# Sixty-four wide tiles in an attention recurrence with segment memory: output products in one pass, scores in one tile shape, a new order of the work

## The chip, the core and the metric

The kernel runs on one core of one Trainium2 chip. TensorE (PE in the profile, with PEld for its weight loads) multiplies, VectorE (DVE), ScalarE (ACT) and GpSimd (POOL) do the rest, and SyncE (SP) issues most of the transfers. The metric is the device time in microseconds of one execution; lower is better.

## The reference

All tensors are bfloat16. The sequence has 2048 tokens of 640 channels, cut into 64 segments of 32 tokens. Each segment is put behind 8 memory tokens, and attention with 32 heads of 192 channels runs over these 40 rows. The first 8 rows of its output are the memory of the next segment, so the segments form a chain. Beside it runs a gated feed-forward layer over all tokens, and a gate mixes the two.

```python
def _A_ref(x, mem0, Wq, Wk, Wv, Wo, seg_len):
    ...
    idx = jnp.arange(L)
    mask = (idx[:, None] < M) | (idx[:, None] >= idx[None, :])
    mem = mem0
    outs = []
    for s in range(n_seg):
        xs = x[:, s * seg_len:(s + 1) * seg_len, :].copy()
        h = jnp.concatenate([mem, xs], axis=1)
        q = jnp.einsum('btd,dhe->bhte', h, Wq)
        k = jnp.einsum('btd,dhe->bhte', h, Wk)
        v = jnp.einsum('btd,dhe->bhte', h, Wv)
        scores = jnp.einsum('bhqe,bhke->bhqk', q, k) * scale
        scores = jnp.where(mask[None, None], scores, -1000000000.0)
        p = _softmax(scores, axis=-1)
        o = jnp.einsum('bhqk,bhke->bhqe', p, v)
        o = jnp.einsum('bhte,hed->btd', o, Wo)
        mem = o[:, :M, :].copy()
        outs.append(o[:, M:, :])
    return jnp.concatenate(outs, axis=1)
...
g = _sigmoid((x * gate_w).sum(-1, keepdims=True))
a = _A_ref(x, A_mem0, A_Wq, A_Wk, A_Wv, A_Wo, A_seg_len)
b = _B_ref(x, B_w_gate, B_w_up, B_w_down)
return g * a + (1 - g) * b
```

## The kernel before

**Stages.** The feed-forward layer comes first (the lines up to 830 or so, some 175 us with the first left rows); its result waits in a scratch tensor. Then the 64 segments run, one after the other. Every operation goes through a recorder (`_Sched`): it lists operations with the regions that they read and write, and derives all waits from these. Each engine runs its own list in order, so the order in which operations are recorded is the order of every queue: TensorE's, VectorE's, ScalarE's, GpSimd's and SP's.

**Rows.** A segment has 40 rows, but a 32-wide tile of TensorE holds 32. The kernel therefore keeps 32 *main* rows (8 memory tokens and the first 24 tokens) and 8 *left* rows (the last 8 tokens). The left rows do not depend on the chain. Those of four segments make a *group*: 32 left rows, whose Q and K are projected ahead, during the group before (`lf` for the matmuls, `le` for eviction, two transposes on VectorE and a store to a scratch tensor, read back by `stg_load` in the segment that needs it). A segment's place in its group, its number modulo 4, is called its position, `q`.

**Heads.** 32 heads go as four octets. Per octet: projections of Q, K and V, each five steps of K (`g` in the order, `proj`, lines 1046 and 226, four matmuls of 32 rows and 384 columns side by side; line 226 is the form that keeps the weights of the matmul before); eviction by ScalarE (L1066, L1069) and transposes of Q and K by VectorE (`tq` and `tk`, L1080); scores (`sc`, L1087 mask, L1095 and L1100); the softmax (L1112 and L1114 with the scores, `ex` with L1124 to L1131); transposed probabilities (`pt`, L1144 and L1149, evicted by L1162 or L1156 with L1158); their product with V (`pv`, L1177 and L1179, evicted into `uT` by L1188 and L1193); and the product with Wo (`wo`, two halves of two pairs each).

A head has 192 channels. Two heads make a pair of 384 = 3 x 128, so the middle 128 hold the ends of both heads: the scores take two 128-row matmuls and two half-height ones for each pair.

**Output.** The first three octets' products with Wo run as four 32-wide tiles, each with 320 columns (L1206): two pairs of heads times two halves of the columns, summed afterwards by one ScalarE copy (`Zp`, L1212) and two VectorE additions (`Zs`, L1215). The last octet's are four tiles of 160 columns (L1229) in bank `OB2`. `Z evac` (L1371) adds both, and L1375 transposes the result into the next segment's input. In position 3 the same Wo pieces also multiply the group's 32 left rows, gathered from four segments in `uTl`, in bank `LB` (`wo_left`, L1206 as well); the last part of it runs after the transposes. `left_sums` adds the halves in the next segment and mixes the rows.

**Weights.** Of 60 Wq, Wk and Wv pieces and 16 Wo pieces most stay in SBUF. 16 places are shared by two pieces each: 13 pieces of the first and the last octet and 3 Wo pairs. Segments run the octets forwards and backwards in turn. When the first user of a place is done, `swap_loads` records on SP the load of its partner (L599), needed at the end of the same segment. SP also issues the loads and stores of the left rows, of the feed-forward rows and of the output, in the same queue.

**The order** is written out by hand in two lists: `GROUPS`, which projections share a step, and `PROG`, the order of all items of a segment. One `PROG` serves all positions; `lf`, `le` and `vb` items act only in the position that they name.

```python
    def segment(s):
        ...
        for n, item in enumerate(PROG):
            kind, i = item[0], item[1]
            ...
            swap_loads(s, item)
```

Of the kernel before, what the change touches and what calls it, by code (L numbers as in the profile page):

```python
# [230 lines left out]

def _build(nc, A_x, A_mem0, A_Wq, A_Wk, A_Wv, A_Wo, seg_len, w_gate, w_up, w_down,
# [46 lines left out]
    total = int(nc.sbuf_bytes_remaining) - 64  # L279
# [8 lines left out]
    wsA["xs"] = al(KT * XA * 2)  # L288
    wsA["gall"] = al(NSEG * 4)
    wsA["gallL"] = al(32 * 4)  # L290
    wsA["ident"] = al(128 * 2)
    wsA["maskm"] = al(R * 2)
    wsA["elw"] = al(2 * 7 * 16 * 2)
    wsA["XLg"] = 2 * al(KT * 32 * 2)
    NVB, NUB = 2, 2
# [7 lines left out]
    wsB["uT"] = al(NUB * 12 * R * 2)  # L303
    wsB["stats"] = al(2 * 3 * 4 * 4 + 8)
    wsB["p"] = al(4 * 64 * 2)
    wsB["uTl"] = al(NCH * 32 * 2)
# [63 lines left out]
    gallL = fview(wsA_off["gallL"], 128)  # L370
    r_gallL = sreg(wsA_off["gallL"], 128)
# [5 lines left out]
    elw = bview(wsA_off["elw"], 448).rearrange("p (i b r) -> p i b r", i=2, r=16)  # L377
    r_elw = sreg(wsA_off["elw"], 448)
# [4 lines left out]
    r_Ql = sreg(wsB_off["Q"] + 8, 12 * R * 2 - 8)  # L383
    Ks = bview(wsB_off["K"], 12 * R * 2).rearrange("p (s r) -> p s r", r=R)
# [4 lines left out]
    stg_off = (wsB_off["stg"], wsB_off["uT"] + 24 * R)  # L389
    assert 8 * LW <= 24 * R  # L390
# [23 lines left out]
    r_uTp = [[sreg(wsB_off["uT"] + b * UB, 4), sreg(wsB_off["uT"] + b * UB + 4, 4)] for b in range(NUB)]  # L414
    st_f = [[fview(wsB_off["stats"] + (3 * b + i) * 16, 16) for i in range(3)] for b in range(2)]
    r_st = [sreg(wsB_off["stats"] + 48 * b, 48) for b in range(2)]
    uTl = bview(wsB_off["uTl"], NCH * 64).rearrange("p (c t) -> p c t", t=32)
    r_uTl = [sreg(wsB_off["uTl"] + 12 * 64 * b, 12 * 64) for b in range(NOCT)]
    bz, bzl = [bview(wsB_off[nm], DJ * 2) for nm in ("bz", "bzl")]
    Zt = PT[:, 0:DJ]  # L420
    r_bzlj = [sreg(wsB_off["bzl"], DJ * 2, 32 * j, 32 * j + 32) for j in range(4)]
# [8 lines left out]
    fp_sz = {"xst": 16 * KT * XA * 2, "xls": 4 * KT * 64, "gr": 512 + 4 * NSEG + 128, "gwT": 64}  # L430
# [13 lines left out]
    r_gin = [sreg(o_gr + 512, 4 * NSEG, 32 * j, 32 * j + 32) for j in range(4)]  # L444
    ginL = fview(o_gr + 512 + 4 * NSEG, 128)
# [54 lines left out]
    def piece_view(key, o):  # L500
        if key[0] == 3:
# [3 lines left out]
    GROUPS = [[(0, 0), (1, 0)], [(2, 0), (0, 1), (1, 1)], [(2, 1), (0, 2)], [(1, 2)], [(2, 2), (0, 3)], [(1, 3)], [(2, 3)]]  # L505
    PROG = [("g", 0, 0), ("g", 0, 1), ("g", 0, 2), ("g", 0, 3), ("g", 0, 4), ("tq", 0), ("g", 1, 0), ("tk", 0),
# [27 lines left out]
    def seg_order(s):  # L534
        keys = []
        for item in PROG:
# [6 lines left out]
    orders = [seg_order(0), seg_order(1)]  # L543
# [20 lines left out]
    o = 0  # L564
# [37 lines left out]
    def piece(seg, key):  # L602
        order = orders[seg % 2]
# [42 lines left out]
    def asel(ap, reg, pattern, base, cm, fill):  # L646
# [9 lines left out]
    S_.add("pool", lambda e: e.memset(elw[:, :, 3, :], 1.0), writes=[r_elw])  # L656
    S_.add("pool", lambda e: e.affine_select(out=elw[:, :, 3, :], in_=elw[:, :, 3, :], pattern=[[-64, 2], [-1, 16]],
                                             compare_op=ALU.is_equal, fill=0.0, base=-XA, channel_multiplier=1),
           reads=[r_elw], writes=[r_elw])
# [204 lines left out]
    gate_loads()  # L864
    load_residents(2)

    S_.add("pool", lambda e: e.memset(pl_sb, 0.0), writes=[r_p])
    lb = {}
    LBK = {}

# [600 lines left out]
```

## Time and profile before

| | us |
|---|---|
| median of 3 runs | 1765.19 (1756.74 to 3865.19) |
| the profiled execution, its span | 1765.1 |
| TensorE's clock in it, mean share of full speed | 0.994 |
| L1046 and L226, projections, busy | 723.0 and 595.4 |
| L1206, output products of 320 columns, busy | 293.6 (6144 matmuls) |
| L1229, those of 160 columns, busy | 74.0 (3072) |
| L1095 and L1100, scores, busy | 69.3 and 70.8 (2048 each) |
| L1080, transposes of Q and K on VectorE, busy, mean of one | 270.8, 0.557 |
| L1215, half sums on VectorE, busy | 50.8 (160) |
| L1196, copies of the left rows on GpSimd, busy | 68.3 (256) |
| DMA, mean | 283 GB/s |

A busy time of TensorE is the time in which at least one matmul of the line ran. Matmuls in different columns of the array run beside each other, so the steps from start to start tell more than the lengths. The third run (3865.19) lies far off the other two.

### The profile page before, as it was taken

To read this page: it belongs to the slowest core of one execution; us is meant where nothing else is said; L and a number is where in the kernel's file an instruction comes from. 1 tells how busy PE (TensorE), PEld (TensorE's weight loads), DVE (VectorE), ACT (ScalarE), POOL (GpSimd) and SP (SyncE) were. 2 spreads that over 40 slices of the span, in tenths; PEclk is the share of its full clock that TensorE was granted. 3 is DMA by queue.
4 is the path that set the end of the run, shared out by engine and by line. 5 is a ranking of instruction groups with operands and counts; after the bars stand their busy time and mean duration, and the time that the engine had idled before them with its cause. 6 is when DMAs were issued, how large, how long until landed. Compare 5 with 4: busy or idle time off the path is not lost.

```text
span 1765.1 us, 80301 instructions
## 1 busy us (share of the span) xinstructions
PE 1623.9 (92%) x39162; PEld 809.5 (46%) x31501; DVE 960.0 (54%) x2932; ACT 802.8 (45%) x1835; POOL 320.0 (18%) x1099
## 2 busy tenths in 40 slices
PE   9999999999999999999999989999999998999887
PEld 4554444444444444454444444454444444454444
DVE  2222655556555655555555655555555655655554
ACT  3222544545444544444444544444444544445443
POOL 1100111111112112111212111111211121121211
PEclk9999999999999999999999999999999999999999
DMA  9814987888778887888788887879787886879776
GB/s 335 295 48 157 329 313 250 320 313 288 280 269 311 299 308 253 315 290 319 281 280 293 296 293 250 314 285 323 279 280 275 311 310 241 312 282 327 283 275 238
DMA packets 271311, 499.57 MB, mean 283 GB/s; under 512 B 105304, under 2 KB 132208, under 8 KB 270960
## 3 DMA queue, kind: packets, MB, share of 16 engines
q1 hardware_dynamic: 267832, 491.34, 78.3%
q8 instruction: 276, 4.52, 1.0%
q10 hardware_dynamic: 3128, 3.09, 0.6%
q14 instruction: 75, 0.61, 0.1%
HBM read 473.22 MB, written 21.11 MB: 280 GB/s over the span
## 4 chain that ended last, share of the span: by engine, by line
PE 71%; DVE 15%; DMA 6%; issue 4%; ACT 4%; DVEq 0%; SPq 0%; ACTq 0%
PE ps L1046 20%; PE ps L226 15%; PE ps L1206 8%; DMA arena<-in_A_Wo_dram 5%; PE ps L1177 3%; PE ps L804 3%; PE ps L801 3%; PE ps L884 3%; PE ps L1100 3%; PE ps L819 2%; PE ps L1087 2%; DVE ps L1114 2%; DVE arena L1112 2%; PE ps L1095 2%; PE ps L1229 2%
## 5 line engine op out<-in xcount | busy, mean ns | idle before, releaser
L1046 PE MATMUL ps<-arena 128*32 128x384 bf16 x9940 | 723.0, 329 | 42.4 <-DVE arena L1375 34.4
L226 PE MATMUL ps<-arena 128*32 128x384 bf16 x7680 | 595.4, 328 | 7.9 <-DVE arena L1215 3.5
L1046 PEld LDWEIGHTS ps<-arena 128*32 128x32 bf16 x9940 | 257.5, 97 | 365.3 <-issue 226.0
L1080 DVE STREAM_TRANSPOSE arena<-arena 128x384 bf16<-128x384 bf16 x512 | 270.8, 557 | 150.8 <-ACT arena L1066 149.2
L1066 ACT ACTIVATE arena<-ps 128x384 bf16<-128x384 f32 x512 | 236.2, 489 | 211.6 <-PE ps L1046 196.3
L1206 PE MATMUL ps<-arena 128*32 128x320 bf16 x6144 | 293.6, 301 | 13.9 <-issue 13.4
L1124 ACT ACTIVATE ps<-ps 104x160 f32<-104x160 f32 x256 | 71.9, 281 | 293.4 <-DVE ps L1114 293.4
L1206 PEld LDWEIGHTS ps<-arena 128*32 128x32 bf16 x6144 | 163.5, 97 | 74.0 <-issue 19.4
L1112 DVE TENSOR_REDUCE arena<-ps 104x4 f32<-104x160 f32 x256 | 83.0, 324 | 165.8 <-PE ps L1100 164.6
L941 POOL COPY arena<-arena 128x96 bf16<-128x96 bf16 x256 | 70.3, 275 | 513.4 <-PE ps L1100 444.2
L1188 ACT ACTIVATE arena<-ps 128x480 bf16<-128x480 f32 (+1 forms) x256 | 137.0, 535 | 43.8 <-PE ps L1179 39.6
L1196 POOL COPY arena<-arena 128x96 bf16<-128x96 bf16 x256 | 68.3, 267 | 441.1 <-ACT arena L1188 357.3
L1162 ACT ACTIVATE arena<-ps 128x448 bf16<-128x448 f32 x192 | 104.2, 543 | 96.7 <-PE ps L1149 96.4
L1069 ACT ACTIVATE arena<-ps 128x384 bf16<-128x384 f32 x256 | 125.1, 489 | 20.9 <-PE ps L1046 16.3
L1177 PE MATMUL ps<-arena 128*64 128x160 bf16 x1536 | 123.1, 243 | 12.5 <-ACT arena L1162 6.9
L1126 DVE TENSOR_REDUCE arena<-ps 104x4 f32<-104x160 f32 x256 | 83.0, 324 | 92.5 <-ACT ps L1124 92.5
L1177 PEld LDWEIGHTS ps<-arena 128*64 128x64 bf16 x1536 | 80.8, 109 | 91.6 <-issue 31.7
L884 PE MATMUL ps<-arena 128*32 128x384 bf16 x1280 | 111.4, 330 | 2.2 <-issue 2.0
L1179 PE MATMUL ps<-arena 128*64 128x64 bf16 x1536 | 104.8, 193 | 4.1 <-issue 4.1
L891 DVE STREAM_TRANSPOSE arena<-arena 128x384 bf16<-128x384 bf16 x128 | 73.7, 576 | 31.6 <-ACT arena L889 27.8
L1215 DVE TENSOR_TENSOR arena<-ps,arena 64x160 f32<-64x160 f32 x160 | 50.8, 317 | 72.3 <-ACT arena L1212 61.6
L1114 DVE TENSOR_TENSOR ps<-ps,arena 104x160 f32<-104x160 f32 x256 | 85.0, 332 | 8.8
(84 smaller groups left out, 1819.2 us busy)
## 6 DMA issues: line engine op xcount, KB each, us to landing
arena<-in_A_Wk_dram SPq DMA_DIRECT2D x335, 384.0 KB, 7.1
arena<-in_A_Wv_dram SPq DMA_DIRECT2D x335, 384.0 KB, 9.1
arena<-in_A_Wo_dram SPq DMA_DIRECT2D x205, 480.0 KB, 6.4
arena<-in_A_Wq_dram SPq DMA_DIRECT2D x209, 384.0 KB, 5.4
arena<-left_qk_scratch SPq DMA_DIRECT2D x126, 96.0 KB, 2.8
left_qk_scratch<-arena SPq DMA_DIRECT2D x49, 192.0 KB, 2.3
left_qk_scratch<-arena SPq DMA_DIRECT2D x30, 96.0 KB, 5.7
ffn_b_scratch<-arena ACTq DMA_DIRECT2D x16, 160.0 KB, 4.4
```

What stands on the lines that cost most here:

```text
L226: return e.add_instruction(mybir.InstMatmult(name=nm, start_tensor_calc=like["start"], stop_tensor_calc=stop, tile_size=(128, 32), tile_po ...
L884: fns.append(lambda e, outp=outp, rhs=rhs, j=j: e.matmul(outp, lhs, rhs, start=(k == 0), stop=(k == KT - 1), tile_position=(0, 32 * j)))
L1046: fns.append(lambda e, outp=outp, rhs=rhs, j=j: e.matmul(outp, lhs, rhs, start=(k == 0), stop=(k == KT - 1), tile_position=(0, 32 * j)))
L1066: S_.add("act", lambda e, m=m, bk=bk: e.activation(out=rows_sb[m], in_=ps[:, bk, 0:384], func=ACTF.Copy), reads=[r_ps[bk]], writes=[r_rows ...
L1069: S_.add("act", lambda e, i=i, bk=bk: e.activation(out=v_sb[i % NVB].rearrange("p (c n) -> p c n", c=3), in_=ps[:, bk, 0:384].rearrange("p ...
L1080: S_.add("dve", lambda e: e.transpose(out=dst[:, :, 0:L], in_=rows_sb[m].rearrange("p (c r) -> p c r", r=L)), reads=[r_rows[m]], writes=[r ...
L1112: S_.add("dve", lambda e: e.tensor_reduce(out=mxs, in_=S3, axis=AX.X, op=ALU.max), reads=[rb], writes=[rst], name="smax max")
L1114: S_.add("dve", lambda e: e.tensor_tensor(out=S3, in0=S3, in1=mxb, op=ALU.subtract), reads=[rb, rst], writes=[rb], name="smax sub")
L1177: return [lambda e: e.matmul(full, v[:, e0:e0 + 64], PTm[:, i], start=True, stop=False, tile_position=(0, 64 * i), skip_group_check=True), ...
L1179: lambda e: e.matmul(part, vl[:, e0:e0 + 64], PTl[:, i], start=False, stop=True, tile_position=(0, 64 * i), skip_group_check=True)]
L1188: S_.add("act", lambda e: e.activation(out=apx(u[:, 0, 0, :], [[R, na], [3 * R, 4], [1, R]]), in_=ps[:, A, 0:na * W].rearrange("p (c t r) ...
L1206: fns.append(lambda e, i=i, t=t, j=j, gv=gv: e.matmul(ps[32 * j:32 * j + 32, bank, 0:2 * DJ].rearrange("p (h n) -> p h n", h=2), lhs2[i], ...
```

## The change

**Scores.** The half-height matmuls ran in 64x64 tiles, one on the upper and one on the lower 64 rows. Now both are 128x64 tiles like the other scores. The upper one is issued with 64 rows of operands in a 128x64 tile (`_matmul_rows`). The lower one has all 128 rows, with `Qz` as its weights: a copy of Q's lower half by GpSimd, with zeros above it.

**Output products.** In position 3, main and left rows share one pass (`wo_both`): 64 weights (32 main, 32 left rows, side by side in `U3`), two tiles of 128x64 with 320 columns each. `U3l` on GpSimd puts the left rows there. Each bank row then holds a finished sum, so `Zp` and `Zs` fall away in position 3, and four operations take the place of the half sums of the left rows (`left_sums`). `Zq evac` (two by VectorE, two by ScalarE) gathers the main rows. In the other positions `Zs` is recorded after the last `pv` instead of before it. `uTl` now holds the left rows of three positions (24 columns), and left rows are loaded and stored in two parts, since their order in the bank changed.

**Order.** Six projection groups instead of seven: K of octet 2 joins V 1 and Q 2. Position 3 has an order of its own, `PROG3`. Both lists are new.

```diff
+def _matmul_rows(e, out, lhsT, rhs, start, stop, tile_position):
+    nm = e.bass.get_next_instruction_name()
+    return e.add_instruction(mybir.InstMatmult(
+        name=nm, start_tensor_calc=start, stop_tensor_calc=stop, tile_size=(128, 64), tile_position=tile_position,
+        bass_skip_group_check=True, ins=[e.lower_ap(rhs), e.lower_ap(lhsT)], outs=[e.lower_ap(out)]))
...
-    GROUPS = [[(0, 0), (1, 0)], [(2, 0), (0, 1), (1, 1)], [(2, 1), (0, 2)], [(1, 2)], [(2, 2), (0, 3)], [(1, 3)], [(2, 3)]]
+    GROUPS = [[(0, 0), (1, 0)], [(2, 0), (0, 1), (1, 1)], [(2, 1), (0, 2), (1, 2)], [(2, 2), (0, 3)], [(1, 3)], [(2, 3)]]
...
+    PROG = [("g", 0, 0), ("g", 0, 1), ("g", 0, 2), ("g", 0, 3), ("g", 0, 4), ("tq", 0), ("g", 1, 0), ("g", 1, 1),
+            ("tk", 0), ("g", 1, 2), ("sc", 0), ("g", 1, 3), ("ex", 0), ("g", 1, 4), ("g", 2, 0), ("g", 2, 1),
+            ("g", 2, 2), ("lf", 1, 0, 0), ("pt", 0), ("tq", 1), ("tk", 1), ("sc", 1), ("g", 2, 3), ("g", 2, 4),
+            ("tq", 2), ("ex", 1), ("lf", 2, 1, 0), ("lf", 1, 0, 1), ("lf", 1, 0, 2), ("pv", 0), ("g", 3, 0),
+            ("tk", 2), ("g", 3, 1), ("g", 3, 2), ("g", 3, 3), ("pt", 1), ("lf", 2, 1, 1), ("g", 3, 4), ("sc", 2),
...
+            ("pt", 3), ("lf", 0, 1, 2), ("wo", 2, 1), ("pv", 3), ("lf", 1, 1, 4), ("lf", 0, 1, 3), ("lf", 0, 1, 4),
+            ("le", 0, 1, 0), ("lf", 2, 1, 4), ("le", 2, 1, 0), ("le", 0, 1, 1), ("le", 1, 1, 0), ("le", 1, 1, 1),
+            ("wo", 3, 0), ("le", 2, 1, 1), ("wo", 3, 1)]
...
+            ("tk", 1), ("g", 2, 1), ("g", 2, 2), ("g", 2, 3), ("g", 2, 4), ("sc", 1), ("tk", 2), ("g", 3, 0),
+            ("pt", 0), ("tq", 2), ("g", 3, 1), ("g", 3, 2), ("g", 3, 3), ("ex", 1), ("pv", 0), ("g", 3, 4),
...
+            ("wo", 2, 0), ("g", 5, 4), ("wo", 2, 1), ("pv", 3), ("vb", 0), ("vb", 1), ("vb", 2), ("wo", 3, 0),
+            ("wo", 3, 1), ("vb", 3), ("vb", 4)]
+    PROGS = (PROG, PROG, PROG, PROG3)
...
+        if m == 0:
+            S_.add("pool", lambda e: e.tensor_copy(
+                out=Qz[64:128], in_=Qs[64:128].rearrange("p (t c) r -> p t c r", c=3)[:, :, 1, :]),
+                reads=[r_Qm, r_Ql], writes=[r_Qz], name="Qz s%d o%d" % (s, o))
...
-            for gp in (0, 64):
-                fns.append(lambda e, gp=gp, c=3 * tl + 1, tl=tl: e.matmul(
-                    ps[gp:gp + R, bank, SC + tl * R:SC + (tl + 1) * R], Qs[gp:gp + 64, c, :], Ks[gp:gp + 64, c, :], start=False,
-                    stop=True, tile_position=(gp, gp), skip_group_check=True))
...
+            c = 3 * tl + 1
+            fns.append(lambda e, c=c, tl=tl: _matmul_rows(
+                e, ps[0:R, bank, SC + tl * R:SC + (tl + 1) * R], Qs[0:64, c, :], Ks[0:64, c, :], False, True, (0, 0)))
+            fns.append(lambda e, c=c, tl=tl: e.matmul(
+                ps[64:64 + R, bank, SC + tl * R:SC + (tl + 1) * R], Qz[:, tl, :], Ks[:, c, :], start=False, stop=True,
+                tile_position=(0, 64), skip_group_check=True))
...
+        if q == 3:
+            u, ru = U3, r_U3p
+            S_.add("pool", lambda e: e.tensor_copy(
+                out=U3.rearrange("p t c r -> p (t c) r")[:, :, R:64], in_=uTl[:, 12 * oc:12 * oc + 12, :]),
+                reads=[r_uTl[oc]], writes=r_U3p[2], name="U3l s%d o%d" % (s, o))
...
+    def wo_both(s, item):
+        for p in wo_pairs(s, item):
+            g_, rg_ = piece(s, (3, p))
             for c in range(3):
...
+                S_.add("pe", [lambda e, i=i, g_=g_, c=c, p=p: e.matmul(
+                    ps[64 * i:64 * i + 64, LB, 0:2 * DJ], U3[:, p % 4, c, :], g_[:, c, 2 * DJ * i:2 * DJ * (i + 1)],
+                    start=(p == NWP - 1 and c == 0), stop=(p == 0 and c == 2), tile_position=(0, 64 * i),
+                    skip_group_check=True) for i in range(2)],
+                    reads=[rg_, r_U3], writes=[r_ps[LB]], name="Wb s%d p%d" % (s, p))
...
     def left_sums(g):
-        half_sums(LB, "left g%d" % g)
-        mix_left(g)
+        for j in range(4):
+            lo = 32 * j
+            S_.add("dve", lambda e, j=j, lo=lo: e.scalar_tensor_tensor(
+                out=bzl[lo:lo + 32], in0=ps[64 * (j // 2) + 32:64 * (j // 2) + 64, LB, DJ * (j % 2):DJ * (j % 2 + 1)],
+                scalar=gallL[lo:lo + 32, g:g + 1], in1=bzl[lo:lo + 32], op0=ALU.mult, op1=ALU.add),
+                reads=r_bzlj[j] + [r_gallL, r_lbq[2 * (j // 2) + 1]], writes=r_bzlj[j], name="mixl2 g%d" % g)
...
+                if i == NOCT - 1 and q < 3:
+                    half_sums(OB, "s%d" % s)
...
-                if q == 3 and item != items[-1]:
-                    wo_left(s, held)
...
+        if q == 3:
+            for j in (0, 2, 1, 3):
+                dst, src = Zt[32 * j:32 * j + 32], ps[64 * (j // 2):64 * (j // 2) + 32, LB, DJ * (j % 2):DJ * (j % 2 + 1)]
+                if j < 2:
+                    S_.add("dve", lambda e, dst=dst, src=src: e.tensor_copy(out=dst, in_=src),
+                           reads=[r_lbq[0]], writes=[r_PTq[j]], name="Zq evac s%d" % s)
+                else:
+                    S_.add("act", lambda e, dst=dst, src=src: e.activation(out=dst, in_=src, func=ACTF.Copy),
+                           reads=[r_lbq[2]], writes=[r_PTq[j]], name="Zq evac s%d" % s)
```

More of the change, by code (lines that the diff above doesn't have):

```diff
@@ L535, in seg_order @@
         keys = []
-        for item in PROG:
+        for item in PROGS[s % 4]:
             if item[0] == "g":
@@ L541, in seg_order @@
         return keys
-    orders = [seg_order(0), seg_order(1)]
+    orders = [seg_order(s) for s in range(4)]
     assert len(orders[0]) == len(set(orders[0])) == 3 * KT * NOCT + NWP
@@ L655, in _build @@
     S_.add("pool", lambda e: e.memset(elw, 0.0), writes=[r_elw])
[L656 to L659, printed above, removed]
+    for i in range(2):
+        S_.add("pool", lambda e, i=i: e.memset(elw[:, 3 + 4 * i, :], 1.0), writes=[r_elw])
+        S_.add("pool", lambda e, i=i: e.affine_select(out=elw[:, 3 + 4 * i, :], in_=elw[:, 3 + 4 * i, :], pattern=[[-1, 16]],
+                                                      compare_op=ALU.is_equal, fill=0.0, base=-XA - 64 * i, channel_multiplier=1),
+               reads=[r_elw], writes=[r_elw])
     for b in (7, 5, 6):
@@ L1263, in _build @@
[L1263 to L1267 removed]
+    mids, n_wos = set(), []
+    for x, prog in enumerate(PROGS):
+        at = prog.index
+        g_end = {mi: at(("g", n, KT - 1)) for n, ms in enumerate(GROUPS) for mi in ms}
+        assert g_end[(2, 1)] < at(("wo", 0, 0))
+        assert at(("sc", 2)) < at(("pv", 1))
+        assert all(at(("wo", i, 1)) < at(("pv", i + (1 if x == 3 else 2))) for i in range(NOCT - (1 if x == 3 else 2)))
+        n_wos.append(at([item for item in prog if item[0] not in ("lf", "le", "vb")][-1]))
+        for u in range(2):
+            if ("le", x, u, 1) not in prog:
+                continue
+            if at(("le", x, u, 0)) < at(("wo", 2, 0)):
+                mids.add((x, u))
+                assert max(at(("sc", 2)), at(("tk", 2)), at(("pv", 1))) < at(("le", x, u, 0))
+                assert at(("le", x, u, 1)) < min(g_end[(1, NOCT - 1)], g_end[(2, NOCT - 1)], at(("sc", 3)))
+            else:
+                assert at(("le", x, u, 0)) > max(at(("wo", 2, 1)), at(("pv", 3)), at(("sc", 3)))
+                assert x < 3 or at(("le", x, u, 0)) > at(("wo", 3, 1))
```

180 lines of the change are left out of this document (92 added, 88 removed), and 20 rows, old and new, of tables (PROG, PROG3).

## The prediction

> **What bounds the kernel now.** I read the page first, then TensorE's waits, then the timeline of single segments, then the busy time of a segment in stretches.
>
> ```profile
> span 1765.1 us, 80301 instructions
> PE 1623.9 (92%) x39162; PEld 809.5 (46%) x31501; DVE 960.0 (54%) x2932; ACT 802.8 (45%) x1835; POOL 320.0 (18%) x1099
> ```
>
> TensorE is busy 92%, but this hides waits, since a matmul that runs beside others counts as busy. The waits of TensorE name the rest (total, times, longest):
>
> ```profile
> PE ps L1046 <- DVE arena L1375: 34.4, 48, 1.2
> PE ps L1144 <- DVE arena L1131: 25.0, 65, 0.7
> PE ps L1206 <- issue: 13.4, 14, 2.0
> ```
>
> First the end of a segment (the new memory tokens are transposed, L1375, before the next projections), then the softmax (L1131) ahead of the transposed probabilities, then pauses in which nothing visible is awaited. So I took starts, not busy times, from TensorE's timeline (start, length, line):
>
> ```profile
> 1002.02 0.34 PE L226 MATMUL ps<-arena 128*32 128x384 bf16 x4
> 1002.28 0.25 PE L1087 MATMUL ps<-arena 128*40 128x160 bf16 x2
> 1002.37 0.26 PE L1095 MATMUL ps<-arena 128*40 128x40 bf16 x8
> 1002.56 0.27 PE L1100 MATMUL ps<-arena 64*40 64x40 bf16 x8
> 1002.76 0.35 PE L884 MATMUL ps<-arena 128*32 128x384 bf16 x4
> 1002.93 0.34 PE L226 MATMUL ps<-arena 128*32 128x384 bf16 x4
> ```
>
> Four 32-wide projection matmuls side by side take 0.163 us start to start. Before a 64-wide group the step is 0.265: a change of tile shape costs 0.10 us. The scores use three shapes in a row: their 16 matmuls take 0.39 us, of which the eight 128x64 ones take 0.10 (four pairs, 0.025 apart) and the rest is a change, the 64x64 half and the change back.
>
> The memory is the second limit (stretch; busy time of each engine; clock; DMA share; GB/s), in a segment that starts at 598.5:
>
> ```profile
> 606.50:610.50 4.00, 4.00 (x114) 1.85 (x78) 2.20 (x8) 2.27 (x6) 0.54 (x3) 1.00 1.02 399
> 610.50:614.50 4.00, 3.54 (x90) 1.92 (x84) 2.74 (x9) 2.60 (x8) 0.80 (x3) 1.00 1.03 404
> 618.50:622.50 4.00, 3.52 (x103) 1.92 (x84) 2.20 (x6) 2.60 (x6) 0.74 (x3) 1.00 0.54 195
> ```
>
> The weight swaps fill the queues at about 400 GB/s from some 4 to 20 us into a segment and are done 2 to 4 us before its end.
>
> By the position of a segment in its group of four (0 to 3) the periods, between the transposes of L1375, have means 25.0, 25.1, 23.4 and 25.2 us. Adding start-to-start steps over the program's order gives TensorE alone, without waits: 21.8, 21.1, 19.3, 21.8. So some 3.2 to 4.1 us of each segment are waits.
>
> **Part by part** (us over the whole program, the profiled run being 1765.1; the clock was at 0.994, and the profiled time equals the median of the runs, 1765.19).
>
> *Scores.* Eight pairs at 0.025 and one change back (0.10) make 0.30 instead of 0.39: 256 x 0.093 = -23.8. The row that carries this is the first eight matmuls of the same group, where a pair of 40-wide matmuls starts 3 ns apart and the next pair 25 ns later. [...] Bound: 0 if the half-height matmul (64 partitions in a 128x64 tile) still makes TensorE change.
>
> *Output products.* Position 0 to 2: unchanged matmuls. In position 3 the old 18 + 24 groups of 320 columns (0.136 each, L1206) and 12 of 160 (0.069, L1229) are 6.5 us; the new 48 pairs of 320 columns are 48 x 0.136 = 6.5. Two 64-wide matmuls side by side for 160 columns take 0.072 in the L1177 group, so 320 in 0.136 follows: 0. What changes is shape: runs of 64-wide work per segment go from 7, 8, 7, 7 to 6, 6, 7, 10, at 0.20 each: (-1 -2 +0 +3) x 0.2, nil to -4.6 by exact steps. Both parts together: 21.1, 20.3, 18.9, 21.9 per position without waits, -29.
>
> *Weight loads.* The six groups keep one more set of weights (20 fewer loads a segment). Groups with kept weights (L226) and without (L1046) both step 0.163: 0.
>
> *Softmax waits.* Last score matmul to first pT was never under 2.27 us (2.17 for the last octet): the chain L1112, L1114, L1124, L1126, L1128, L1130, L1131. The old order has 1.4 to 2.4 us of work there in many places; the stalls ahead of pT add to 54. In the new order the work is 2.5 to 4.3 nearly everywhere, 2.13 in two places (0.08 each); in position 3 pT of octet 1 has two transposes (0.56 each) queued ahead of its sum on VectorE: 0.28. 16 x 0.44 = 7 remain: -47. Bounds -54 and -20.
>
> *What is late next.* The new order puts Tq 1 and Tk 1 straight before scores 1. Both stand behind the first softmax on VectorE: 2.22 (up to the end of L1131) + 2 x 0.56 + gaps = 3.45 us after scores 0, against 2.84 to 3.3 us of TensorE work in positions 0 to 2: +0.1, +0.4, +0.6. Bank reuse behind ScalarE's evictions (0.489 each, three in a row after a three-piece group) adds about 0.4 in position 2. The waits for PV change from 0.8 to 0.4 per four segments, scores 3 by +0.1. Sum +1.3 x 16 = +20.
>
> *The copy Qz* (GpSimd, 64x160): rows of 128x96 take 0.27 and 128x120 0.29, so about 0.33. It lies beside Tk (0.56) except once, in position 3: 0. If uncovered at every score it is 256 x 0.4 = +102. U3l (288 elements) about 0.4, ends long before its Wb: 0.
>
> *Left sums.* In position 0 bank LB is needed 1.26 us after scores 0. The old Zp runs beside the scores and two Zs (0.32) free the bank: 0.41 stall. Now four 32x160 operations on VectorE, nearest rows 0.32 to 0.39, follow max and subtract (0.94) and all read the bank: free at about 2.4, stall 1.14. +0.73 x 16 = +12 (bounds +8, +15).
>
> *Ends.* Position 0 now has both left transposes (L891, two of 0.57) ahead of Za on VectorE, as positions 1 and 2 had: PV to next projection 2.8 becomes 3.05 although TensorE has less to do there: +0.6. Position 3: two Zq of 0.3 replace one Z evac of 0.24, 12 left groups no longer cover it, two vb groups do: +0.3. +0.9 x 16 = +14. In positions 1 and 2 this tail stays.
>
> *Pauses named issue.* 34 in all, mostly 1.2 to 2.4 us long and in position 3; the longest begin 0.2 to 1.7 us after a 16 KB packet on the instruction queue (q8) starts and end 2.3 to 2.9 after it. There the old order issues 216 output matmuls with as many loads; the new has 96. I take -16; bounds 0 and -28.
>
> *DMA.* As many swaps (16 a segment). In position 1 the last Wo piece lands 23.3 us after the segment's start, 0.4 before use: TensorE waits for it (a stall of 0.5). Its swaps start 1.1 us late, since a store behind a left transpose that ran after the boundary holds SP's queue; that transpose now comes earlier. So the landing moves to about 22.2 and the need to about 22.1; the wait lies beside the left transposes: -9, bounds -9 and +43 (below). The 126 more DMA issues of the split left rows (0.3 to 0.5 us of SP each) come behind the Wo swaps; ahead of the loads for the next segment, which have slack: 0, bound +10.
>
> Sum: -29 -47 +20 +12 +14 -16 -9 = -55. I keep 4 of it back for waits of octet 1's kind that this sum does not hold: -51, so 1714.
>
> **Rivals.**
>
> *The weights set the time* (no change). The third Wo piece is freed 1.3 and 1.6 us later in positions 1 and 2 (after 15.6 and 14.2 us of work, before 14.3 and 12.6) and its successor is needed sooner. For: 400 GB/s until the end. Against: the last landing was 5.3 us or more behind its release, so it is queue and not release that sets it. If landings (22.2 and 21.0) move with the release: 23.5 and 22.6, plus 0.4, 0.2 and 0.9 to the next segment, 25.0 and 24.1 against my 23.5 and 22.9: 16 x 2.7 = +43, 1757. Chance 0.17.
>
> *The scores still change shape* (the change does not do what it says): +24, 1738. For: the 64-row matmuls of L1100 do make it. Against: pT at 104 rows (L1144) does not. 0.06.
>
> *The waits come back elsewhere*: what the softmax gave, VectorE's order takes: +48, 1762. For: the octet-1 finding. 0.10.
>
> *Slower: 64-wide tiles of 320 columns do not run side by side*, or two 64-column weight loads (0.109 each, L1177) show. Place: Wb in position 3; price 768 x 0.136 = +104, 1818; it decides from half of that on, where all my gain is gone. Against: L1177's pairs start 3 ns apart with the same loads. 0.05.
>
> **Numbers.** My forecast, 1714, has 0.62, own range 1685 to 1740. 2% is about what a measurement of this kernel can tell from no change; that is 1730. Faster: 0.57 of the forecast's cases and 0.03 of the others, 0.60. Same: 0.05 + 0.13 + 0.06 + 0.06 = 0.30. Slower, 0.10: the tiles (0.05), and the worst of weights and waits. The range reaches from the sum with the instruction pauses and softmax at their better bounds (1765 - 55 - 12 - 7 = 1691, and 6 for TensorE's unnamed waits, which I left as they were) to the weights' case: 1685 to 1758.
>
> **What would show it.** Scores to the next group at 0.30; L1100's successor in the same shape as L1095's. Nearly no wait of pT on L1131. New waits of the second scores on L1080's successor, most in position 2. In position 0 the bank's wait above 1 us. Pauses named issue well under 34. Periods near 24.8, 23.5, 22.9, 24.3. I am wrong if TensorE waits on in_A_Wo in most segments, or if Wb steps by more than 0.14.

## The result, and the profile after

| | before | after |
|---|---|---|
| median of the runs, us | 1757.9 (20 runs, 1754.2 to 3865.2) | 1752.1 (20 runs, 1737.0 to 1761.0) |
| ratio, 95% interval | | 0.996 [0.9941, 0.9979] |
| span of the profiled execution, us | 1765.1 | 1748.7 |
| period of a segment by position 0 to 3, mean, us | 25.0, 25.0, 23.4, 25.3 | 24.7, 24.4, 23.3, 25.0 |
| the same, forecast | | 24.8, 23.5, 22.9, 24.3 |

The change makes the kernel 0.4% faster, clear of the noise, where 1714 us and 3% had been forecast. (Periods here run from the first projection of a segment to that of the next, over 15 groups of four.)

The page after: its span, and the busy time of each engine.

```profile
span 1748.7 us, 75451 instructions
PE 1598.3 (91%) x37242; PEld 779.9 (45%) x28301; DVE 968.4 (55%) x2918; ACT 783.0 (45%) x1835; POOL 413.6 (24%) x1358
```

TensorE lost 26 us of busy time, the span only 16: the share of idle time rose. TensorE's waits after (total, times, longest):

```profile
PE ps L1077 <- DVE arena L1448: 47.9, 63, 1.3
PE ps L226 <- DVE arena L1345: 17.9, 15, 1.2
PE ps L1278 <- DMA arena<-in_A_Wo_dram: 12.9, 20, 2.7
PE ps L1278 <- issue: 12.4, 12, 1.9
PE ps L1077 <- DMA arena<-in_A_Wk_dram: 8.4, 16, 0.7
PE ps L1077 <- DMA arena<-in_A_Wv_dram: 7.5, 21, 0.6
PE ps L1130 <- DVE arena L1111: 4.5, 17, 0.4
```

The softmax, 25.0 before, is gone from the list. In its place stand the end of the segment (L1448 is the old L1375; 34.4 before), bank LB behind the left sums (L1345), and the landing of weights, 29 us over three tensors. Before it was little more than this line:

```profile
PE ps L1229 <- DMA arena<-in_A_Wo_dram: 6.1, 10, 2.3
```

The pauses named issue fell from 34 to 20.5 us over all lines. Before, 21.6 of them lay in position 3; there the profile after has none, but positions 0 to 2 have more.

The scores in TensorE's timeline (start, length, line):

```profile
412.98 0.26 PE L1130 MATMUL ps<-arena 128*40 128x40 bf16 x8
413.08 0.18 PE L234 MATMUL ps<-arena 64*40 64x40 bf16 x1
413.09 0.18 PE L1137 MATMUL ps<-arena 128*40 128x40 bf16 x1
...
413.17 0.18 PE L1137 MATMUL ps<-arena 128*40 128x40 bf16 x1
413.27 0.35 PE L1077 MATMUL ps<-arena 128*32 128x384 bf16 x4
```

16 matmuls in eight pairs some 25 ns apart, and the next group 0.29 us after the first: no change of shape shows between L1130 and L234, which start 0.10 us apart, as four pairs take. The median of all score groups is 0.293, before 0.396.

The weights' transfers in a segment of position 1 that starts at 600.7, in stretches of 8 to 12, 12 to 16, 16 to 18 and 18 to 22 us (last columns: clock, DMA share, GB/s):

```profile
608.71:612.71 4.00, 4.00 (x118) 1.71 (x76) 2.28 (x8) 2.77 (x7) 0.82 (x4) 1.00 0.93 347
612.71:616.71 4.00, 3.99 (x108) 1.90 (x82) 3.04 (x9) 2.39 (x7) 1.03 (x4) 1.00 1.04 402
616.71:618.71 2.00, 1.76 (x62) 1.14 (x54) 1.12 (x3) 1.04 (x3) 0.00 (x0) 1.00 1.10 355
618.71:622.71 4.00, 3.85 (x106) 2.24 (x98) 2.18 (x9) 2.75 (x8) 0.82 (x4) 1.00 0.88 318
```

The stream is full until 16 us, then sags, while pieces are still to come. Over all segments of position 1 it carries 280 and 308 GB/s in the 17th and 18th us (before 355 and 316), of position 2 332 and 345 (before 395 and 396).

### The profile page after: what moved, and what is told of

It reads as the page before. It is cut to its first block, busy times and chain, and to the rows that moved or that the text cites. A ratio compares the mean times of both kernels' runs of the same rounds, so it can differ in the third digit from the quotient of the medians.

```text
span 1748.7 us, 75451 instructions
## 1 busy us (share of the span) xinstructions
PE 1598.3 (91%) x37242; PEld 779.9 (45%) x28301; DVE 968.4 (55%) x2918; ACT 783.0 (45%) x1835; POOL 413.6 (24%) x1358
## 4 chain that ended last, share of the span: by engine, by line
PE 39%; DMA 13%; DVE 5%; issue 2%; ACT 2%; POOL 1%; POOLq 0%; SPq 0%; DVEq 0%; ACTq 0%
PE ps L1077 12%; PE ps L226 11%; DMA arena<-in_A_Wv_dram 6%; DMA arena<-in_A_Wo_dram 5%; PE ps L1296 4%; PE ps L1253 3%; DMA arena<-in_A_Wk_dram 3%; PE ps L1217 2%; PE ps L1122 2%; PE ps L914 1%; DVE arena L921 1%; DVE arena L1345 1%; PE ps L1130 1%; PE ps L1278 1%; ACT arena L1100 1%
## 5 line engine op out<-in xcount | busy, mean ns | idle before, releaser
L1077 PEld LDWEIGHTS ps<-arena 128*32 128x32 bf16 x8660 | 222.8, 96 | 462.6 <-issue 268.2
L1111 DVE STREAM_TRANSPOSE arena<-arena 128x384 bf16<-128x384 bf16 x512 | 274.5, 561 | 153.9 <-ACT arena L1097 153.7
L1097 ACT ACTIVATE arena<-ps 128x384 bf16<-128x384 f32 x512 | 230.4, 492 | 260.8 <-PE ps L1077 249.4
L1114 POOL COPY arena<-arena 64x160 bf16<-64x160 bf16 x256 | 82.0, 320 | 424.8 <-DVE arena L1111 415.8
L1253 PE MATMUL ps<-arena 128*32 128x320 bf16 x3456 | 178.8, 299 | 2.3 <-ACT arena L1196 0.6
L1100 ACT ACTIVATE arena<-ps 128x384 bf16<-128x384 f32 x256 | 125.0, 488 | 109.5 <-PE ps L1077 107.9
L971 POOL COPY arena<-arena 128x96 bf16<-128x96 bf16 x256 | 70.5, 275 | 238.1 <-PE ps L1137 157.0
L1296 PE MATMUL ps<-arena 128*64 128x320 bf16 x1536 | 122.7, 302 | 1.1 <-ACT arena L1235 0.9
L1217 PE MATMUL ps<-arena 128*64 128x160 bf16 x1536 | 118.1, 240 | 3.7 <-issue 3.7
L1253 PEld LDWEIGHTS ps<-arena 128*32 128x32 bf16 x3456 | 95.2, 96 | 50.8 <-ACT arena L1196 12.7
L1243 POOL COPY arena<-arena 128x96 bf16<-128x96 bf16 x192 | 51.7, 269 | 273.9 <-ACT arena L1235 266.1
L1217 PEld LDWEIGHTS ps<-arena 128*64 128x64 bf16 x1536 | 81.4, 109 | 47.4 <-ACT arena L1100 19.7
L1296 PEld LDWEIGHTS ps<-arena 128*64 128x64 bf16 x1536 | 79.2, 109 | 30.9 <-issue 8.5
```

Source lines behind the costliest of these rows:

```text
L1077: fns.append(lambda e, outp=outp, rhs=rhs, j=j: e.matmul(outp, lhs, rhs, start=(k == 0), stop=(k == KT - 1), tile_position=(0, 32 * j)))
L1097: S_.add("act", lambda e, m=m, bk=bk: e.activation(out=rows_sb[m], in_=ps[:, bk, 0:384], func=ACTF.Copy), reads=[r_ps[bk]], writes=[r_rows ...
L1100: S_.add("act", lambda e, i=i, bk=bk: e.activation(out=v_sb[i % NVB].rearrange("p (c n) -> p c n", c=3), in_=ps[:, bk, 0:384].rearrange("p ...
L1111: S_.add("dve", lambda e: e.transpose(out=dst[:, :, 0:L], in_=rows_sb[m].rearrange("p (c r) -> p c r", r=L)), reads=[r_rows[m]], writes=[r ...
L1217: return [lambda e: e.matmul(full, v[:, e0:e0 + 64], PTm[:, i], start=True, stop=False, tile_position=(0, 64 * i), skip_group_check=True), ...
L1253: fns.append(lambda e, i=i, t=t, j=j, gv=gv: e.matmul(ps[32 * j:32 * j + 32, bank, 0:2 * DJ].rearrange("p (h n) -> p h n", h=2), lhs2[i], ...
```

## The experiments

Each was compared with the kernel before on its own chip; the medians of before there were 1761 to 1767.

**1. Weight swaps left out, and the scores put back.** Theory A: the weight train hides the gain. Theory B: VectorE, banks and tails took it. Theory C: the score change saves nothing.

```diff
-            load_piece(other, "swap s%d" % seg)
+            loaded[slot_id[other]] = other
```

> The changed kernel without the 16 weight swaps of a segment (1008 loads less; the places keep their first pieces, so the products of the last or first octet use other weights). Theory A (the weight train hides the gain): the stalls of TensorE on Wo, Wk and Wv, some 50 us, go: about 1700 us. Theory B (VectorE, banks and tails took the gain): only the 15 us that the kernel before has too go: about 1738.

> The kernel before, also without the 16 swaps of a segment. Both theories: its own weight stalls (Wo 8 us, a little more behind it) go: about 1740 to 1748. What decides is the difference changed minus before with both without swaps: theory A -40 to -50 us, theory B -5 to -15.

> The changed kernel with the half-height scores in 64x64 tiles as before, no Qz. My step of 0.093 us for each of 256 score groups: 24 us of work come back. Theory A: where the train sets the time this shows in part: +5 to +15 us. Theory B: +24. Theory C (the score change saves nothing): 0.

> The changed kernel without swaps and with the half-height scores in 64x64 tiles. Against the run without swaps alone: theories A and B +24 us, since nothing hides the work; theory C 0.

| | us | ratio to before, interval |
|---|---|---|
| changed, no swaps | 1688.7 | 0.958 [0.9559, 0.9601] |
| before, no swaps | 1700.4 | 0.9651 [0.9627, 0.9675] |
| changed, old scores | 1763.0 | 1.0002 [0.9976, 1.0027] |
| changed, no swaps, old scores | 1717.5 | 0.9743 [0.9722, 0.9764] |

TensorE's waits of the changed kernel without swaps:

```profile
PE ps L1077 <- DVE arena L1448: 57.5, 63, 1.3
PE ps L226 <- DVE arena L1345: 17.9, 15, 1.2
PE ps L1130 <- DVE arena L1111: 8.8, 29, 0.4
```

and of the kernel before without swaps:

```profile
PE ps L1046 <- DVE arena L1375: 34.0, 48, 0.9
PE ps L1144 <- DVE arena L1131: 27.3, 64, 0.7
```

Theory A falls as put: the difference of the two kernels without swaps is -12 us, not -40 to -50, as theory B has it. But neither theory expected that the swaps cost the kernel before as much: they cost both kernels about 60 us. The waits of the kernel before name 6 of it for Wo and 34 as pauses. In neither kernel is one pause named issue left without swaps. Theory C falls: without swaps the scores alone give 28.8 us (1717.5 to 1688.7). So everything else in the change, order and output products, costs 17 us there (1700.4 to 1717.5), and with swaps it comes out at nothing.

With swaps the same change of the scores gives only some 7 us (1.0002 to 0.996; by the two intervals 2 to 13), which fits theory A (5 to 15) and not B (24): the traffic takes back some 21 of the 29. In the profiles, one for each version, the pauses named issue go from 9.3 us with the old scores to 20.5 with the new ones, and the waits for weights from 21 to 29.

**2. The same traffic, but nobody waits for it.** The swap loads write to 16 places that no matmul reads.

```diff
+    alias = {(2, o, k): (2, o, 0) for o in (1, 2) for k in range(1, KT)}
...
-            load_piece(other, "swap s%d" % seg)
+            S_.add("sp", lambda e, n=n, other=other: e.dma_start(piece_view(other, spare_off[n]), piece_src(other)),
+                   writes=[r_res[key], sreg(spare_off[n], piece_size(other))], dma_sem="dum%d" % n, ...)
```

> The changed kernel with all swap loads issued at the same place, by the same releases and of the same size, but into 16 places that no matmul reads (for that, 16 resident weights are replaced by their neighbours): the traffic stays, no matmul waits for a landing. Without swaps it took 1689, with them 1752. Theory D (the landings cost): only the 20 us of instruction pauses stay: about 1710. Theory E (the traffic itself costs, by pauses and slower transfers and stores): 1730 to 1750.

> The kernel before with the same edit. Without swaps it took 1700, with them 1758 to 1763. Its pauses named issue are 34 us, its named waits for weights 8. Theory D: 1734 and the rest of the loss in landings that the waits do not name; theory E: 1745 to 1755. The difference to the changed kernel with the same edit, if the landings are what took the expected gain: 20 to 30 us; otherwise about 10.

Measured: 1749.9 (0.993 [0.9903, 0.9956]) and 1778.1 (1.0097 [1.0066, 1.0127]). These totals can't be used as they are: the edit delays the start (the first segment begins at 185.9 and 184.7 us instead of 177.5 and 177.1 in the changed kernel and the one before, and TensorE waits some 12 us for weights in it). The periods of the later segments can, summed over four positions, times 16:

| us | before | changed |
|---|---|---|
| with swaps | 98.74 | 97.42 |
| traffic without landings | 97.93 | 96.07 |
| no swaps | 94.77 | 93.73 |
| so: landings x 16 | 13 | 22 |
| so: traffic alone x 16 | 51 | 37 |

Theory E holds for the larger part: the traffic costs most of the 60 us without any wait for a weight. The pauses named issue are 33 of the 51 and 26 of the 37; the rest carries no name. But the landings cost the changed kernel 9 us more than the kernel before, where I had 9 less. One profile each stands behind these numbers.

**3. Places freed earlier; SP's queue freed.** First the first half of octet 0's output products is moved up in positions 0 to 2, then the stores of left rows are taken out of the way of the swaps (`pend` holds those of the middle of position 1 until the next item is recorded).

```diff
-            ("wo", 0, 0), ("tq", 3), ("g", 4, 3), ...
+            ("tq", 3), ("g", 4, 3), ...
...
-            ("tk", 2), ("g", 3, 1), ("g", 3, 2), ("g", 3, 3), ("pt", 1), ("lf", 2, 1, 1), ("g", 3, 4), ("sc", 2),
+            ("tk", 2), ("g", 3, 1), ("g", 3, 2), ("g", 3, 3), ("pt", 1), ("lf", 2, 1, 1), ("g", 3, 4), ("wo", 0, 0), ("sc", 2),
```

> The changed kernel, with the first half of the first octet's output products moved up in positions 0 to 2, from before tq 3 to straight behind projection group 3: two Wo places are free some 3 us earlier, so that the queue does not run low at 15 to 18 us. If the landing of the last Wo piece depends on these releases (the rival of the prediction): landing 1 to 1.5 us earlier in positions 0 to 2, and 10 to 20 us less. If the queue's rate sets it: landing unchanged, time within 3 us.

```diff
-            left_store(g, o, 3)
+            left_store(g, o, 3, "act")
...
+            if pend and item[0] != "le":
+                pend.pop(0)()
```

> The changed kernel; the stores of the left rows no longer hold SP's queue: the late ones go by ScalarE's queue, the two of the middle of position 1 stand behind the swap of the Wo pieces. Swaps start 0.3 us earlier in position 1 and 0.7 in position 3, the Wo pieces of position 1 are asked for 0.4 us earlier. If the start of the train sets the waits for weights (Wk in position 3, Wo in 1): 5 to 12 us less. If the pauses do: within 3 us.

Measured: 1754.3 (0.9971 [0.9949, 0.9992]) and 1767.2 (1.003 [1.0005, 1.0055]): no gain over the changed kernel's 0.996, and in the second a loss (at a clock of 0.987). The landing did move: the last Wo piece came at 21.1, 21.8 and 20.7 us in positions 0 to 2 (21.8, 22.8 and 21.5 in the changed kernel), and of the waits for Wo 0.2 us is left in the first run. But a new wait of TensorE stands there:

```profile
PE ps L1253 <- ACT arena L1196: 21.6, 24, 2.3
```

In the second run the same wait is 33.4 us:

```profile
PE ps L1253 <- ACT arena L1196: 33.4, 21, 3.6
```

Both stand in position 1, ahead of PV 3 (1.6 and 2.3 us in place of 0.32). There the store of the left rows reads the buffer that V of octet 3 goes to; both edits put it behind weight swaps, and V's eviction (L1100) waits for it, 0.7 us in all in the changed kernel. ScalarE's waits in the first run

```profile
ACT arena L1100 <- DMA left_qk_scratch<-arena: 27.4, 12, 3.2
```

and in the second:

```profile
ACT arena L1100 <- DMA left_qk_scratch<-arena: 45.0, 15, 4.5
```

In position 2, which has no such store, the period fell by 0.38 us with the early products. So the landing of the last Wo piece does hang on when the Wo places are freed, against my prediction (in the first run two of the three were free 1.6 to 2.7 us earlier, the third within 0.4 us of the changed kernel); and the left store is one more user of that queue that TensorE waits for.

**4. Ends and bank.** The left sums at the end of position 3, with swaps and without; and both left evictions of position 0 behind the last output product.

```diff
-                if i == 0 and q == 0 and g > 0:
-                    left_sums(g - 1)
...
-        if s + 1 == NSEG:
+        if q == 3:
             left_sums(g)
```

> The changed kernel with the four left sums at the end of the segment in position 3 instead of behind scores 0 of the next: bank LB is free before Q of octet 2 needs it, the 1.37 us wait of position 0 (21.7 in all) goes. If nothing is late behind it: -20 us. If the last Wo piece of position 0, which lands 1.5 us ahead of its use, is next: -15 to -20. If the weights set the period there: 0 to -5.

> The changed kernel without swaps and with the left sums at the end of position 3. With swaps the sums moved this way gave about 12 us of the 21.7 that the wait on bank LB takes. Theory: the other 9 are taken back by landings and pauses; then without swaps the whole 20 to 22 us shows (1689 to about 1668). If VectorE takes it back elsewhere: 10 to 14 us here too.

```diff
-            ("wo", 3, 0), ("le", 2, 1, 1), ("wo", 3, 1)]
+            ("wo", 3, 0), ("le", 2, 1, 1), ("wo", 3, 1), ("le", 0, 1, 0), ("le", 0, 1, 1)]
```

> The changed kernel without swaps, with both left evictions and transposes of position 0 behind the last output product instead of ahead of it. The wait between segments after position 0 is 1.47 us with them ahead and was 0.87 in the kernel before, with one behind: if they are its cause, 0.6 x 16 = -9 us (to about 1679); if not, within 2 us.

Measured: left sums with swaps 1742.4 (0.9889 [0.9859, 0.992]), some 12 us better than the changed kernel's ratio, less than the 15 to 20 put; without swaps 1674.7 (0.9498 [0.9459, 0.9537]), 14 less than 1688.7. The bank's wait goes in both, but 6 to 7 us come back right behind it, without any traffic: the left V of octet 1 waits for the bank of the Q and K rows (0.48 us, position 0). The waits of the run without swaps:

```profile
PE ps L1077 <- DVE arena L1446: 57.4, 63, 1.2
...
PE ps L1077 <- ACT arena L1097: 4.6, 15, 0.3
```

The evictions of position 0: 1679.1 (0.9524 [0.9477, 0.9571]), 9.6 less. That is as much as the 0.6 x 16 of the prediction: those two transposes make the end longer there. Of the 9.6, 7.1 us stand in the wait at the ends, which falls from 57.5 to

```profile
PE ps L1077 <- DVE arena L1448: 50.4, 63, 1.0
```

**5. The clock.** Over all runs the granted clock of the changed kernel had a median of 0.993 (0.988 to 0.999), that of the kernel before 0.998 (63 runs beside the experiments, 0.992 to 1.000). Time and clock go together: a straight line through the 20 runs of the changed kernel gives 1740 us at full clock and 1935 us for each unit of clock lost, through the 63 of before 1759 and 1632. By these lines the lower clock costs 13.5 and 3.3 us. Stretches of the changed kernel's trace around one low spot (busy time of the engines, then clock, DMA share, GB/s):

```profile
935.60:939.00 3.40, 2.22 (x65) 1.14 (x55) 2.02 (x5) 1.64 (x4) 0.46 (x2) 1.00 0.54 180
939.00:942.40 3.40, 1.23 (x27) 0.52 (x19) 1.20 (x5) 0.00 (x0) 1.12 (x3) 1.00 0.35 92
942.40:945.80 3.40, 3.40 (x52) 0.68 (x16) 1.04 (x2) 0.87 (x2) 0.60 (x3) 0.51 0.81 239
945.80:949.20 3.40, 3.40 (x94) 0.98 (x42) 1.89 (x7) 1.45 (x4) 0.53 (x2) 0.99 0.95 308
```

At the end of a segment TensorE works 1.23 of 3.4 us (it waits 1.8 us in a pause named issue ahead of the last output products and 0.63 us for the transpose of L1448); in the next 3.4 us it gets half the clock and gets through 52 matmuls where the stretch behind it has 94. The test: fill the waits between segments with matmuls that nobody reads.

```diff
+        for n in range((6, 6, 6, 3)[q] if s + 1 < NSEG else 0):
+            S_.add("pe", [lambda e, j=j, fb=fb: e.matmul(ps[32 * j:32 * j + 32, fb, 0:384], ...) for j in range(4)],
+                   reads=[...], writes=[r_ps[fb]], name="fill s%d" % s)
```

> The changed kernel with idle TensorE time filled between segments: 6 groups of 4 matmuls (0.98 us) behind the last output product in positions 0 to 2 and 3 groups in position 3, into a free bank, read by nobody. TensorE waits there 1.2 to 1.5 us (0.8) anyway. The granted clock was 0.993 in the median of the changed kernel's runs and 0.997 to 0.998 in those of the kernel before; in the traces each half-clock stretch of 3.4 us follows a stretch of 3.4 us in which TensorE was busy for 0.56 or less. If that is the rule: clock at 0.997 or above, and 6 to 11 us less. If power or the traffic sets the clock: clock as before or lower, and time the same or longer.

Measured: clock 0.9975 (0.994 to 0.999) in 12 runs, where 0.997 or above was put; but 1767.5 us (1.0013 [0.9987, 1.004]), 9 us more than the changed kernel's ratio gives, not 6 to 11 less. The profiles, one of each, show two places of the loss. The filling (54 us) doesn't quite fit into the waits: from the last useful matmul of a segment to the first projection of the next it is 70.6 us over the 63 ends, 64.0 without filling. In positions 0 to 2 the projection starts 0.15 us after the transpose that it waits for, without filling 0.06. And the pauses named issue are 27.3 us after 20.5. The waits for weights in sum stay at 29 us. From the list with filling:

```profile
PE ps L1077 <- DMA arena<-in_A_Wk_dram: 11.4, 19, 1.6
PE ps L1278 <- issue: 9.1, 10, 1.6
PE ps L1077 <- DMA arena<-in_A_Wv_dram: 9.1, 23, 0.7
```

So the clock rose with the idle time filled (0.9975, without filling 0.993), and what the filling costs is in part its own length. Why the pauses grow is not shown: the run has 1332 more matmuls and ten more instruction packets (266 for 256 on q8) beside the same traffic, and nothing here separates them.

The longer ends alone did not lower the clock. Without swaps the changed kernel has its longest ends (57.5 us), and still:

```profile
core 0: 1686.9 us, clock 0.999
```

No 3.41 us stretch from 220 us to its last matmul has TensorE busy for less than 0.60. With swaps the profile has ten such stretches, and in each TensorE waits for a Wo piece or in a pause named issue ahead of the last output products, in eight of them beside the 0.6 us at the segment's end.

**6. Together.** Four versions from the parts above: left sums early, late left stores on ScalarE's queue, early output products in position 2 only; the first of them also with the stores of position 1 put off, the last two with the filling, the last with the evictions of position 0 behind.

> Three edits together: left sums at the end of position 3 (about -12 alone), the stores off SP's queue, and the early half of the first output products in position 2 only, where it took 0.38 us off the period. If they add: -12 -8 -6, about 1726 and a ratio to before of 0.98. If one limit is behind all three: about -15.

> The changed kernel with the left sums at the end of position 3, the late left stores by ScalarE's queue, and the first half of the first output products early in position 2; unlike the run before, the stores of the middle of position 1 stay where they were, since their delay held V of octet 3 there (2.3 us ahead of PV 3). Alone: -12, about -6 (positions 0, 2, 3) and -6. If these add: 1728 to 1735. If the clock falls further with every idle stretch that gets no shorter: 1740 to 1745.

> As the run with the three edits, and with the filled idle time between segments. If idle stretches set the clock, 6 to 11 us less than without: 1720 to 1728, a ratio to before of about 0.98. If not, the same time as without.

> As the run before, and with both left evictions of position 0 behind the last output product (-9.6 us without swaps), with 3 groups of filling there in place of 6. If ends of segments add to the rest: about 1712 to 1720. If the landing of the weights in position 1 sets the time there: within 4 us of the run before.

| | us | ratio, interval |
|---|---|---|
| with the stores of position 1 put off | 1755.9 | 0.9955 [0.993, 0.998] |
| without that | 1731.4 | 0.9812 [0.9766, 0.9857] |
| the same, filled | 1744.3 | 0.9881 [0.9851, 0.991] |
| filled, position 0 as without swaps | 1813.4 | 1.0268 [1.022, 1.0317] |

The second beats both kernels: 1.9% below before, where the change alone gives 0.4%. What is left in it, waits of TensorE:

```profile
PE ps L1079 <- DVE arena L1448: 49.7, 63, 1.3
PE ps L1280 <- DMA arena<-in_A_Wo_dram: 9.3, 18, 2.0
PE ps L1079 <- DMA arena<-in_A_Wv_dram: 8.7, 20, 0.8
PE ps L1079 <- DMA arena<-in_A_Wk_dram: 7.4, 13, 0.7
```

The filling costs 13 us here as well; the ends grow from 65.8 to 72.2 us and the pauses named issue from 14.1 to 32.0. In the fourth, ScalarE itself stands still, since the eviction of V (here L1102) waits for a store of left rows, and TensorE behind it:

```profile
ACT arena L1102 <- DMA left_qk_scratch<-arena: 53.8, 15, 6.0
PE ps L226 <- ACT arena L1102: 56.4, 15, 6.2
```

What gave 9.6 us without swaps costs over 60 with them, by the same coupling as in experiment 3.

## Why the prediction was wrong

It said -51 us; the medians say -6. By its own steps, measured without swaps where the step has no part in them:

| step | forecast, us | measured, us |
|---|---|---|
| softmax waits | -47 | -51 (61.5 to 10.1) |
| late next (scores, K's bank, PV) | +20 | +23 |
| bank LB | +12 | +14 (1.37 us each) |
| ends | +14 | +23 (34.0 to 57.5) |
| TensorE's own work | -29 | about -21, what the other lines leave of -12 |
| all without traffic | -30 | -12 |
| pauses named issue | -16 | -13 |
| landings of weights | -9 | +9 |
| clock | not in the sum | +10 |
| sum | -55, 4 kept back | -6 |

The stalls are sums over the trace; the line without traffic is the difference of medians in experiment 1. The spans of its two profiles differ by 16. Pauses and landings are from one profile each, the clock from the medians. So it is no proof that the column adds up to -6: its lines come from different runs, and TensorE's own work is a remainder that takes up the errors of the others. Nor do the parts simply add: the 29 us of the scores without traffic are 7 with it.

**Right.** Scores: the step went from 0.396 to 0.293, and without swaps the scores alone give 28.8 us instead of 23.8, since 81 of the 256 groups now run straight into the 64-wide PV, 0.22 us after their start, with no change of shape at all. In the timeline above the matmuls in two column tiles start in pairs, a pair some 25 ns after the one before. The new groups of output products and the copy Qz on the page after (busy, mean ns; then idle time before them):

```profile
L1114 POOL COPY arena<-arena 64x160 bf16<-64x160 bf16 x256 | 82.0, 320 | 424.8 <-DVE arena L1111 415.8
...
L1296 PE MATMUL ps<-arena 128*64 128x320 bf16 x1536 | 122.7, 302 | 1.1 <-ACT arena L1235 0.9
```

Qz takes 0.32 us, as put, and is hidden. The output products step at 0.136 (the first of each item 0.160), so the rival of the 64-wide tiles falls, and with the scores' step that of the change of shape. Softmax, the waits that follow it, bank LB and the pauses are each within 4 us. (The terms listed for the waits that follow add to 1.2 us, not 1.3; that is under 2 us of the sum.) For the pauses this is partly luck: those of position 3 went, as put, but all 21.6 us of them, and 8 us came back in positions 0 to 2, of which the prediction has nothing. Over the versions of the changed kernel with swaps, one profile each, they range from 9.3 to 32.0 us.

**The step that failed: DMA.** I wrote that the landing in position 1 "moves to about 22.2", for -9, because "it is queue and not release that sets it". Measured: 22.8 there, and in position 2 21.5 after 21.0. The first swap did start 0.8 us earlier in position 1, as forecast. But the third Wo place was freed 1.4 and 1.3 us later in positions 1 and 2 (16.6 and 15.8 us into the segment); the stream ran low at 16 to 18 us and the gain was gone. In position 1 the queue did run ahead, the last Wv piece landed 18.0 us into the segment after 19.4. But the last Wo load was issued at 16.8 in both kernels: in SP's queue a store of left rows that waits for its transpose (until 14.5 us, 14.8 before) stands ahead of the Wo loads, so the release of the third place was not alone in holding them there. In position 2, without such a store, the load was issued at 16.0 after 14.5. The full stretches that I showed of the kernel before end 16 us into the segment, and the gap that a late release leaves comes behind them; in position 1 it was there already. Experiment 3 shows it: with two of the three places freed 1.6 to 2.7 us earlier, the last piece landed 0.7 to 1.0 us earlier. This is the mechanism of the rival "the weights set the time". Its price of +43 was too high, since landings followed only part of the delay in release, but its 1757 is the nearest of the cases. The prediction's own sign, a wait for Wo in most segments, did not appear: it is 20 of 63, all but one of them in positions 1 and 2. In position 3, which I left out, K of octet 3 waited in 16 segments (8.4 us by the waits), with swaps that start at 1.2 instead of 0.5 us.

**Mis-sized: ends.** From the last output product to the next projection, without swaps, position 0 got 0.5 us longer (0.6 put; 9.6 us came back in experiment 4). Positions 1 and 2, "this tail stays", got 0.2 us longer each, and position 3 0.6 instead of 0.3. Why 1 and 2 did was not tried; there the half sums now come after the last PV and stand with both left transposes ahead of Za on VectorE.

**Missing: the clock.** I took it as 0.994 on both sides; the medians of the runs, 0.993 and 0.998, are worth some 10 us. By experiment 5 the lower clock comes from landings and pauses next to the ends of segments, not from the longer ends alone (0.999 without swaps, where they are longest), so it is a price of the traffic too. Where a typical run of the kernel before differs is not shown: its one profile has 0.994, the changed kernel's 0.995.

## What to carry to other kernels

Leave the transfers out for one run of both kernels: it splits a change into what it does on the engines and what the traffic takes back, in runs most of which agree to 1 us. What a part gives without the traffic need not show with it (28.8 and 7 us for the scores). A full queue proves nothing about a later release: find the time from which a release would leave it empty (here some 16 us into the segment), and who else waits in the same queue. And idle time of TensorE had two prices here: its length, and the clock after it (half clock after 30 of 30 full-clock stretches of 3.41 us with TensorE busy for under 0.45, after none of 7728 above 0.60). By these counts it should cost more gathered in one stretch than spread out; no run tested that alone.

## What the runs showed of the hardware

- **Pauses named issue came with the traffic.** 34 and 20.5 us of pauses named issue with the weight stream, none in either kernel without it, at as many instruction packets (256 on q8 in the changed kernel, with and without). Traffic that nobody waits for brought them back (33 and 26 us).
- **Half the clock after a stretch that is not idle, only slack.** In the profiles of both kernels every change of the granted clock falls on a grid of 3.41 us, between full clock and half. In the 18 profiles, from 220 us on, a stretch at full clock with TensorE busy for under 0.45 was followed by half clock in 30 of 30 cases, one with 0.45 to 0.60 in 27 of 106, and one above 0.60 never (7728). Of the stretches at half clock themselves, 3 of 60 above 0.60 were followed by another. The busiest of the full-clock stretches that half clock followed had TensorE busy for 0.57. In the lines shown above, 1.23 of 3.4 us busy is followed by a clock of 0.51, with 52 matmuls where the next 3.4 us have 94.
- **The tile's shape changed the pace, not the rows of the operands.** Matmuls with 64 rows of operands (L234) in a 128x64 tile run beside 128-row ones, in pairs some 25 ns apart, and a score group takes 0.293 us; with the same 64 rows in 64x64 tiles it took 0.396, 0.10 us more a time.
